# Own buffers for the last three output parts, and a margin before transposes and PV matmuls in the planner's first batch

## Chip, cores and metric

The kernel runs on one core of one Trainium2 chip. The metric is the device time of one execution in microseconds (us), the median of three. A profile of one execution, taken on the same chip, gives a span that is a little shorter than the device time; times inside the trace count from the start of that span.

## What is computed

Block-sparse attention (batch 4, 8 heads, sequence 768, head width 64) and then an MLP-mixer layer on its output. Cut to what matters:

```python
# attention, per batch and head; mask = neighbouring blocks, first and last block, 3 sampled blocks
scores = np.where(mask, q @ k.T / 8, -1e9)
attn = exp(scores - max) / sum
x = attn @ v                          # [4, 768, 512] once the heads stand side by side
# token mixing
u = x + (relu(x.T @ w_tok1) @ w_tok2).T      # 768 -> 256 -> 768, over the sequence
# channel mixing
out = u + relu(u @ w_ch1) @ w_ch2            # 512 -> 1536 -> 512, over the channels
```

Inputs and output are float32; the kernel works in bfloat16 with float32 sums.

## The kernel before

The heads are worked off as 16 pairs (`p` = 0 to 15, four pairs to a batch). For each pair:

- `k`, `q` and `v` are loaded with conversion to bfloat16 (GpSimd's queue, L230, tiles `kraw`, `qraw`, `vraw`), and VectorE rearranges them (L524 `klay`, `qlay`; L521 `vaug`).
- TensorE transposes `klay` and `qlay` (`tk`, `tq`, L575, six matmuls each, for pairs 1 to 9; later pairs use the DMA's transposing path), and VectorE or ScalarE copies the result to `ktb` and `qtb` (L604, or L589 from pair 6 on).
- Nine score steps `(t, jj)` follow. Each has matmuls of keys by queries into the PSUM tile `ps` (L633), one exponential by ScalarE over 128x1024 elements into `et` (L643), and eight PV matmuls of `et` by `vaug` into `po` (L719). After three steps VectorE normalizes (L733 `recip`, L734 into `x`).
- In pairs 0 to 5 the mask rides inside the score matmul as 24 additional rows of `ktb` and `qtb`. From pair 6 on VectorE multiplies `et` by a 0/1 tile `mask` (L651). That tile is built in between by twelve matmuls `pm_mask` (L484) and twelve comparisons (L492).

When two pairs of a batch are complete, token mixing of half the channels runs (`pm_tok`, L797 and L822; VectorE adds into `x`, L830). The result is transposed (`pm_ut`, L851, in the first batch). When a batch is complete, channel mixing runs: 96 matmuls L889 per batch, ReLU into `rc` (L761 ScalarE or L763 VectorE), and the second product L915, which VectorE adds to `u` and stores in `o` (L924, or L931 for partial widths). SyncE's queue writes `o` to memory (L935).

The order on every engine is fixed when the kernel is built. A `Planner` runs a clock of its own (`now`, in ns) over estimated costs. It has streams for TensorE, in order of priority: scores 0, PV 1, mask 1.8, transposes 2, token mixing 3, channel mixing 4. At each moment the first stream whose next item is ready, by the planned times of its inputs and by free PSUM buffers, is put next on TensorE. VectorE, ScalarE and SyncE take from a list of operations in the same way. The planned times only choose an order: on the chip each engine works through its list in that order and waits, by semaphores, for what an instruction really needs. If an instruction's input comes later than planned, everything behind it on its engine waits too.

Buffers that matter here: `ps` 2, `po` 1, `pm` 3 (PSUM, shared by transposes, mask, token and channel mixing), `et` 7, and three rotating output tiles `o`. In the last batch the last 128 rows of the output are cut by channels into parts of 256, 128 and 128, so that only a small piece is left after the last matmul. These parts take their tiles from the same three `o` buffers:

```python
parts[-1:] = [(NC - 1, 0, 256), (NC - 1, 256, 128), (NC - 1, 384, 128)]
...
o = sbw.tile([128, DM], FP32, tag="o", bufs=3, name=f"o{b}_{sc}_{lo}")
```

The functions that the diff touches:

Of the kernel before, what the change touches and what calls it, by code (L numbers as in the profile page):

```python
# [8 lines left out]
FP32 = mybir.dt.float32  # L9
# [41 lines left out]
class Planner:  # L51
# [6 lines left out]


    PE_LAT, SEM = 180.0, 50.0  # L60
    trace = None

    def __init__(self, slots):
# [39 lines left out]
    def step(self):  # L103

        nxt = []
        moved = False
        if self.free_at["pe"] <= self.now:
            for s in self.streams:
                while s[3] is None or (callable(s[3]) and s[3]()):
                    s[3] = next(s[2], False)  # L110
                if s[3] is False or callable(s[3]):
                    continue
                cost, deps, tags, emit, done = s[3]
                t = self.when(deps, tags)
                if t is None:
                    continue
                if t <= self.now:
                    s[3] = None
                    emit()
                    if self.trace is not None:  # L120
                        self.trace.append((self.now, "pe", s[0], cost))
                    self.free_at["pe"] = self.now + cost
                    if done is not None:
                        done.t = self.now + cost + self.PE_LAT + self.SEM
                    moved = True
                    break
                nxt.append(t)
            self.streams = [s for s in self.streams if s[3] is not False]
        else:
            nxt.append(self.free_at["pe"])  # L130
        for eng in ("act", "dve", "sp"):
            if self.free_at[eng] > self.now:
                nxt.append(self.free_at[eng])
                continue
            best = None
            for o in self.ops:
                prio, num, engines, cost, deps, emit, done, lat, tags = o
                if eng not in engines:
                    continue
                if eng == "act" and prio > 0 and self.exp_pending:  # L140
                    continue
                t = self.when(deps, tags)
                if t is None:
                    continue
                if t <= self.now:
                    if best is None or (prio, num) < best[:2]:
                        best = o
                else:
                    nxt.append(t)
            if best is not None:  # L150
                prio, num, engines, cost, deps, emit, done, lat, tags = best
                self.ops.remove(best)
                emit(eng)
                c = cost[eng]
                if self.trace is not None:
                    self.trace.append((self.now, eng, prio, c))
                self.free_at[eng] = self.now + c
                done.t = self.now + c + lat + self.SEM
                moved = True
        if moved:  # L160
            return True
        later = [t for t in nxt if t > self.now]
        if not later:
            return False
        self.now = min(later)
        return True
# [3 lines left out]
def kernel(  # L170
# [17 lines left out]
    DM, DT, DC = 512, 256, 1536  # L188
# [9 lines left out]
    sbw = ctx.enter_context(tc.tile_pool(name="sbw", bufs=2))  # L198
# [13 lines left out]
    P = Planner({"ps": 2, "po": 1, "pm": 3, "et": NET, "a_t": 2, "o": 3, "rc": 2,  # L212
                 "uT": 3})
# [158 lines left out]
    def first_turn(nm, hf):  # L372
        t = psM.tile([128, 3, 128], BF16, tag="pm", name=f"t{nm}first{hf}")
        for c in range(3):
            nc.tensor.matmul(
                out=t[:, c, :], lhsT=lay0[nm][:, 3 * hf + c, :, :].rearrange("p h d -> p (h d)"),
                rhs=ident[:, :], start=(c == 0), stop=(c == 2), is_transpose=True,
            )
        return t

    def first_evac(copy, nm, hf, hd, t):
        buf = (ktb if nm == "k" else qtb)[0]
        copy(
            out=buf[0:64, hd, 384 * hf : 384 * hf + 384],
            in_=t[64 * hd : 64 * hd + 64, :, :].rearrange("p c s -> p (c s)"),
        )
# [9 lines left out]
    def e2_copy(copy, hf, hd, t):  # L396
        copy(out=qtb[0][R, hd, 384 * hf : 384 * hf + 384], in_=t[R, 0:384])
# [27 lines left out]
    def first_rest():  # L425

        def band(eng):
            nc.vector.tensor_copy(out=ktb[0][R, 1, 384:S], in_=indf[:, 384:S])

        P.op(("dve",), {"dve": 250.0}, [], band, prio=0)  # L430
        for nm in ("k", "q"):
            box, last, rel = {}, Ev(), Ev()

            def emit(nm=nm, box=box, rel=rel):
                P.take("pm", rel)
                box["t"] = first_turn(nm, 1)

            yield 330.0, [Ev(START + (200.0 if nm == "k" else 600.0))], [("pm", 1)], emit, last
            for hd in range(2):
                def evac(eng, nm=nm, hd=hd, box=box):  # L440
                    first_evac(vcopy, nm, 1, hd, box["t"])

                ev = P.op(("dve",), {"dve": 350.0}, [last], evac, prio=0)
                f_there[nm, 1].same_as = ev
                rel.same_as = ev
        box, last, rel = {}, Ev(), Ev()

        def emit():
            P.take("pm", rel)
            box["t"] = e2_mm(1, psM, "pm")  # L450

        yield 330.0, [], [("pm", 1)], emit, last
        for hd in range(2):
            def copy(eng, hd=hd, box=box):
                e2_copy(vcopy, 1, hd, box["t"])

            e2_there = P.op(("dve",), {"dve": 420.0}, [last], copy, prio=0)
            rel.same_as = e2_there
        rows_there[0] = e2_there
        for n in range(1, NV):  # L460
            def spread(eng, n=n):
                if eng == "dve":
                    nc.vector.tensor_copy(out=qtb[n][R, :, :], in_=qtb[0][R, :, :])
                else:
                    nc.sync.dma_start(out=qtb[n][R, :, :], in_=qtb[0][R, :, :])

            rows_there[n] = P.op(
                ("dve",) if n == 1 else ("sp",), {"dve": 560.0, "sp": 800.0}, [e2_there], spread,
                prio=1, lat=60.0 if n == 1 else 5000.0,
            )  # L470
# [401 lines left out]
    def ch(b, pool, tag):  # L872
# [4 lines left out]
        for cc in range(12):  # L877
            for sh in range(2):
                last, rel, pbox = Ev(), Ev(), {}
# [28 lines left out]
        for sc, lo, n in parts:  # L908
            last, rel, pbox = Ev(), Ev(), {}
            for cc in range(12):  # L910
                def emit(sc=sc, cc=cc, lo=lo, n=n, rel=rel, pbox=pbox):
                    if cc == 0:
                        P.take("pm", rel)
                        pbox["pm"] = psM.tile([128, DM], FP32, tag="pm", name=f"pm_ch2_{b}_{sc}_{lo}")
                    nc.tensor.matmul(  # L915
                        out=pbox["pm"][:, 0:n], lhsT=box["rc"][:, cc, 128 * sc : 128 * sc + 128],
                        rhs=w_ch2[:, cc, lo : lo + n], start=(cc == 0), stop=(cc == 11),
                    )
                yield n / 2.4 + 2.5, [rc_there[cc, sc // 3], ch2_there[cc // 3]], [("pm", 1)] if cc == 0 else [], emit, last if cc == 11 else None

            def fin(eng, sc=sc, lo=lo, n=n, pbox=pbox):
                o = sbw.tile([128, DM], FP32, tag="o", bufs=3, name=f"o{b}_{sc}_{lo}")
                if n == DM:
                    nc.vector.tensor_tensor(  # L924
                        out=o[:, :].rearrange("p (g e) -> p g e", g=2),
                        in0=pbox["pm"][:, :].rearrange("p (g e) -> p g e", g=2),
                        in1=st[b]["u"][:, :, sc, :], op=ALU.add,
                    )
                else:
                    g, e = lo // 256, lo % 256  # L930
                    nc.vector.tensor_tensor(  # L931
                        out=o[:, 0:n], in0=pbox["pm"][:, 0:n],
                        in1=st[b]["u"][:, g, sc, e : e + n], op=ALU.add,
                    )
                nc.sync.dma_start(  # L935
                    out=APx(out, b * S * DM + sc * DM + lo, [[NC * DM, 128], [1, n]]),
                    in_=o[:, 0:n],
                )

            alias(rel, P.op(("dve",), {"dve": dve_psum(n)}, [last], fin, prio=3))  # L940
        alias(rc_rel, last)

# [81 lines left out]
```

## Time and profile before

| what | value |
|---|---|
| device time, median of 3 | 265.2 us (265.01 to 265.48) |
| span of the profiled execution | 263.8 us |
| TensorE busy | 254.3 us (96%) |
| ScalarE busy | 178.4 us (68%) |
| VectorE busy | 173.1 us (66%) |
| mean granted TensorE clock | 0.993 of full speed |

Two stages with different limits can be told apart. Up to some 195 us attention runs, with token and channel mixing between the scores where they are ready. In the first batch nothing of channel mixing can be ready yet, and ScalarE, with its exponentials, is the busiest engine (10.00 us busy in the stretch from 20 to 30 us). From some 196 us on only channel mixing is left: long runs of L889 and L915 on TensorE. After the last matmul come one VectorE addition and one write to memory.

### The profile page before, as it was taken

How to read it: one execution, taken by the hardware profiler on the slowest of the kernel's cores; microseconds unless marked ns; L12 is line 12 of the kernel's file. 1: busy time of each engine (PE TensorE's matmuls, PEld its weight loads, DVE VectorE, ACT ScalarE, POOL GpSimd, SP SyncE). 2: the span in 40 equal slices, each digit the busy share in tenths (PEclk: the TensorE clock that was granted, in tenths of full speed). 3: DMA queues.
4: the chain of work that ended last, by engine and by line, in shares of the span. 5: the costliest groups of instructions: out<-in, count | busy, mean ns of one | idle time of the engine just before them, and what ended most of it. 6: DMA issues, size and time to landing. Idle time of an engine off the chain costs nothing.

```text
span 263.8 us, 6585 instructions
## 1 busy us (share of the span) xinstructions
PE 254.3 (96%) x2769; PEld 167.2 (63%) x2787; DVE 173.1 (66%) x387; ACT 178.4 (68%) x226; POOL 42.1 (16%) x66
## 2 busy tenths in 40 slices
PE   7899999999999999999999999999999999999993
PEld 3588886898765676567555765666565644565452
DVE  7978968697989789788879798888850013200221
ACT  5789999998887887677777887777317720277000
POOL 8845555462303010000000000000000000000000
PEclk9899999999999999999999999999999999999999
DMA  6999999999665826141734030016214012300122
GB/s 149 183 217 201 213 202 207 204 199 180 90 93 77 105 32 119 43 102 40 176 94 34 2 60 2 2 40 102 81 42 99 0 42 80 121 2 0 48 111 82
DMA packets 39262, 25.58 MB, mean 97 GB/s; under 512 B 20480, under 2 KB 35600, under 8 KB 39232
## 3 DMA queue, kind: packets, MB, share of 16 engines
q0 software_dynamic: 15104, 12.98, 31.6%
q1 hardware_dynamic: 23856, 11.97, 19.4%
q8 instruction: 22, 0.36, 0.6%
q10 hardware_dynamic: 272, 0.20, 0.3%
q14 instruction: 8, 0.07, 0.1%
HBM read 26.74 MB, written 6.29 MB: 125 GB/s over the span
## 4 chain that ended last, share of the span: by engine, by line
PE 87%; DVE 4%; ACT 3%; DMA 2%; issue 1%; SPq 0%; DVEq 0%; ACTq 0%
PE pm_ch L889 24%; PE pm_ch L915 22%; PE ps L633 17%; PE po L719 13%; PE pm_tok L797 4%; PE pm_tok L822 4%; ACT et L643 3%; DMA out_dram<-o 1%; PE tk L575 1%; DMA kf<-in_k_dram 1%; PE pm_mask L484 1%; DVE x L830 1%; DVE et L651 1%; PE tq L575 1%; DVE o L924 0%
## 5 line engine op out<-in xcount | busy, mean ns | idle before, releaser
L643 ACT ACTIVATE et<-ps 128x1024 bf16<-128x1024 f32 x144 | 138.9, 1023 | 29.9 <-PE ps L633 28.9
L889 PE MATMUL pm_ch<-uT,w_ch 128*128 128x384 bf16 x384 | 70.1, 326 | 0.0
L915 PE MATMUL pm_ch<-w_ch,rc 128*128 128x512 bf16 (+2 forms) x294 | 67.0, 362 | 1.1 <-issue 0.3
L633 PE MATMUL ps<-qtb,ktb 64*128 64x256 bf16 (+1 forms) x576 | 61.2, 274 | 1.4 <-ACT et L643 1.2
L719 PEld LDWEIGHTS <-et 128*128 128x128 bf16 x1152 | 49.9, 98 | 16.3 <-issue 3.0
L651 DVE TENSOR_TENSOR et<-et,mask 128x1024 bf16<-128x1024 bf16 x90 | 57.8, 682 | 0.0
L719 PE MATMUL po<-vaug,et 128*128 128x65 bf16 x1152 | 56.3, 194 | 0.6 <-DVE et L651 0.2
L761 ACT ACTIVATE rc<-pm_ch 128x384 bf16<-128x384 f32 x69 | 33.8, 492 | 26.9 <-PE pm_ch L889 26.7
L924 DVE TENSOR_TENSOR o<-pm_ch,x 128x512 f32<-128x512 f32 x23 | 15.8, 687 | 52.6 <-PE pm_ch L915 52.6
L889 PEld LDWEIGHTS <-w_ch 128*128 128x128 bf16 x384 | 35.4, 98 | 22.0 <-issue 2.2
L633 PEld LDWEIGHTS <-ktb 64*128 64x128 bf16 (+1 forms) x576 | 33.0, 96 | 19.4 <-issue 13.9
L915 PEld LDWEIGHTS <-rc 128*128 128x128 bf16 x312 | 27.5, 97 | 24.8 <-issue 1.3
L733 DVE RECIPROCAL recip<-po 128x4 f32<-128x4 f32 x48 | 8.7, 181 | 20.4 <-PE po L719 20.1
L734 DVE TENSOR_TENSOR x<-po,recip 128x256 bf16<-128x256 f32 x48 | 20.4, 424 | 1.7
L830 DVE TENSOR_TENSOR x<-pm_tok,x 128x512 bf16<-128x512 f32 x24 | 15.6, 682 | 4.1 <-PE pm_tok L822 4.1
L230 POOL DMA_DIRECT2D vraw<-in_v_dram x16 | 11.7, 730 | 34.1 <-DVE vaug L521 29.0
L763 DVE TENSOR_SCALAR rc<-pm_ch 128x384 bf16<-128x384 f32 x27 | 14.8, 552 | 2.2 <-PE pm_ch L889 1.8
L822 PE MATMUL pm_tok<-a_t,w_tok 128*128 128x256 bf16 x96 | 14.6, 276 | 0.2
L797 PE MATMUL pm_tok<-x,w_tok 128*128 128x256 bf16 x96 | 13.4, 273 | 0.0
L230 POOL DMA_DIRECT2D kraw<-in_k_dram x15 | 10.8, 718 | 7.8 <-DMA w_tok<-in_moe_w_tok_dram 2.7
L230 POOL DMA_DIRECT2D qraw<-in_q_dram x15 | 10.8, 723 | 6.6 <-DVE klay L524 1.2
L822 PEld LDWEIGHTS <-w_tok 128*128 128x128 bf16 x96 | 9.8, 128 | 1.6 <-issue 1.2
(70 smaller groups left out, 114.4 us busy)
## 6 DMA issues: line engine op xcount, KB each, us to landing
out_dram<-o SPq DMA_DIRECT2D x23, 256.0 KB, 2.1
vraw<-in_v_dram POOLq DMA_DIRECT2D x16, 192.0 KB, 7.3
w_ch<-in_moe_w_ch_dram POOLq DMA_DIRECT2D x8, 384.0 KB, 9.8
kraw<-in_k_dram POOLq DMA_DIRECT2D x15, 192.0 KB, 7.8
qraw<-in_q_dram POOLq DMA_DIRECT2D x15, 192.0 KB, 7.3
w_tok<-in_moe_w_tok_dram POOLq DMA_DIRECT2D x2, 384.0 KB, 10.9
kf<-in_k_dram SPq DMA_DIRECT2D x2, 192.0 KB, 3.2
ktb<-ktb SPq DMA_DIRECT2D x3, 72.0 KB
```

What stands on the lines that cost most here:

```text
L230: nc.gpsimd.dma_start(out=raw[:, :, :, :], in_=APx(src, 2 * p * S * D, [[NC * D, 128], [S * D, 2], [1, NC * D]]),)
L633: nc.tensor.matmul(out=ps[:, hd, 256 * i : 256 * i + 256], lhsT=ktb[n][rows, h, 256 * jj + 128 * i : 256 * jj + 128 * i + 128], rhs=qtb[n] ...
L643: nc.scalar.activation(out=et[:, :, :], in_=ps[:, :, :], func=AF.Exp, scale=0.125)
L651: nc.vector.tensor_tensor(out=ets[s][:, :, :].rearrange("k h (i q) -> k h i q", i=2), in0=ets[s][:, :, :].rearrange("k h (i q) -> k h i q" ...
L719: nc.tensor.matmul(out=po[:, hd, c, :], lhsT=et[:, hd, 256 * i + 128 * c : 256 * i + 128 * c + 128], rhs=va[:, hd, 2 * jj + i, 0:65], star ...
L734: nc.vector.tensor_tensor(out=free(xs[b][:, pb // 2, 2 * t, 128 * (pb % 2) : 128 * (pb % 2) + 128], 0, [[64, 2], [256, 2], [1, 64]],), in0 ...
L761: nc.scalar.activation(out=o(), in_=i, func=AF.Relu)
L797: nc.tensor.matmul(out=box["pm"][:, t, :], lhsT=w_tok1[:, sc, 128 * t : 128 * t + 128], rhs=xs[b][:, g, sc, :], start=(t == 0 and sc == 0) ...
L822: nc.tensor.matmul(out=ubox["pm"][:, i, :], lhsT=w_tok2[:, t, :, 2 * s2 + i], rhs=a_t[:, t, :], start=(i == 0 and t == 0), stop=(i == 1 an ...
L830: nc.vector.tensor_tensor(out=st[b]["u"][:, g, 2 * s2 : 2 * s2 + 2, :], in0=ubox["pm"][:, :, :], in1=xs[b][:, g, 2 * s2 : 2 * s2 + 2, :], ...
L889: nc.tensor.matmul(out=pbox["pm"][:, 0:384], lhsT=w_ch1[:, dmc, 128 * cc : 128 * cc + 128], rhs=st[b]["uT"][:, dmc // 2, 3 * sh : 3 * sh + ...
L915: nc.tensor.matmul(out=pbox["pm"][:, 0:n], lhsT=box["rc"][:, cc, 128 * sc : 128 * sc + 128], rhs=w_ch2[:, cc, lo : lo + n], start=(cc == 0 ...
```

## The change

There are three edits. The first lets the planner, while its clock is below 40 us, treat items of the streams with priority 1.8 and 2 (mask, transposes) as ready only 300 ns after the planned time of their inputs, and PV items (priority 1) 100 ns after. What is put next in such a moment is whatever else is ready. The second raises the planned VectorE cost of one small copy in the start-up from 420 to 555 ns. The third gives the three partial output tiles a tag of their own with three buffers of 256 columns. The purpose of the first two is an order in which TensorE is held up less by inputs that come late; that of the third is that the last tiles need not wait for earlier ones to be written.

```diff
     PE_LAT, SEM = 180.0, 50.0
+    tight = 40e3
...
                 t = self.when(deps, tags)
                 if t is None:
                     continue
+                if self.now < self.tight:
+
+                    t += 300.0 if 1.5 < s[0] < 2.5 else 100.0 if s[0] == 1 else 0.0
                 if t <= self.now:
...
-            e2_there = P.op(("dve",), {"dve": 420.0}, [last], copy, prio=0)
+            e2_there = P.op(("dve",), {"dve": 555.0}, [last], copy, prio=0)
...
-                o = sbw.tile([128, DM], FP32, tag="o", bufs=3, name=f"o{b}_{sc}_{lo}")
+                if n == DM:
+                    o = sbw.tile([128, DM], FP32, tag="o", bufs=3, name=f"o{b}_{sc}_{lo}")
+                else:
+                    o = sbw.tile([128, 256], FP32, tag="olast", bufs=3, name=f"o{b}_{sc}_{lo}")
```

In the built programs the order changes on TensorE and VectorE from the first transposes of pair 1 up to the transposes `pm_ut` and the token mixing of the first batch (some 70 us in the trace of before). From there on both programs have the same order, except for the output buffers. One copy, `ktb` from the transposes of pair 9, moves from VectorE to ScalarE. The queues of SyncE and GpSimd keep their order. No instruction is added or removed.

## Prediction

> **What bounds the kernel now.** I read four views in this order: the page (engine sums and slices), the chain of waits that ended last, the timelines of the two ends of the kernel, and the waits by engine.
>
> ```profile
> PE 254.3 (96%) x2769; PEld 167.2 (63%) x2787; DVE 173.1 (66%) x387; ACT 178.4 (68%) x226; POOL 42.1 (16%) x66
> PEclk9899999999999999999999999999999999999999
> PE 87%; DVE 4%; ACT 3%; DMA 2%; issue 1%; SPq 0%; DVEq 0%; ACTq 0%
> ```
>
> TensorE is the bound as a whole (87% of the chain). But it is not loaded alike everywhere, and both edits sit at ends where something else decides. First the tail: the timeline from 255 us (start, length, engine, line; in brackets the idle time before and what ended it) and the end of the chain.
>
> ```profile
> 254.78 4.54 PE L915 MATMUL pm_ch<-w_ch,rc 128*128 128x512 bf16 x44
> 256.71 0.69 DVE L924 TENSOR_TENSOR o<-pm_ch,x 128x512 f32<-128x512 f32 x1 [1.90 <-PE pm_ch L915]
> 258.02 0.42 DVE L931 TENSOR_TENSOR o<-pm_ch,x 128x256 f32<-128x256 f32 x1 [0.62 <-PE pm_ch L915]
> 258.69 0.29 DVE L931 TENSOR_TENSOR o<-pm_ch,x 128x128 f32<-128x128 f32 x1 [0.25 <-PE pm_ch L915]
> 260.94 0.29 DVE L931 TENSOR_TENSOR o<-pm_ch,x 128x128 f32<-128x128 f32 x1 [1.96 <-DMA out_dram<-o]
> ```
> ```profile
> 256.71 0.70 DVE o L924
> 257.43 3.39 DMA out_dram<-o
> 260.82 0.03 issue
> 260.85 0.05 DVEq L931
> 260.89 0.04 issue
> 260.94 0.29 DVE o L931
> ```
>
> The last matmul ends at 254.78+4.54 = 259.32, yet the last addition starts at 260.94: it waits for the write of the tile three before it, the 256 KB tile filled at 256.71, which lands at 260.82. The chain goes through that write, not through TensorE. Now the head.
>
> ```profile
> 9.00:10.00 1.00, 0.33 (x2) 0.16 (x2) 0.97 (x3) 1.00 (x2) 0.96 (x3) 1.00 1.24 185
> 11.00:12.00 1.00, 1.00 (x10) 0.82 (x8) 0.94 (x4) 0.71 (x1) 0.66 (x1) 0.50 1.35 201
> 12.00:13.00 1.00, 1.00 (x17) 0.94 (x16) 0.99 (x2) 0.56 (x1) 0.68 (x2) 0.50 1.22 179
> 13.00:14.00 1.00, 1.00 (x17) 0.88 (x15) 0.58 (x4) 0.46 (x1) 0.73 (x2) 0.50 1.34 207
> ```
> ```profile
> 12.44 1.02 ACT L643 ACTIVATE et<-ps 128x1024 bf16<-128x1024 f32 x1 [0.73 <-PE ps L633]
> 14.52 22.45 ACT L643 ACTIVATE et<-ps 128x1024 bf16<-128x1024 f32 x24 [1.06 <-PE ps L633]
> ```
>
> The columns of the first view are the stretch, its length, busy time of PE, PEld, DVE, ACT and POOL, granted clock, DMA share and GB/s. From 11 to 14 us TensorE runs at half clock and ScalarE starves (0.73 and 1.06 us idle, both waiting for score matmuls). Then 24 exponentials run without a gap, 22.45/24 = 0.935 us each: to 37 us ScalarE sets the pace, and TensorE has time to spare.
>
> **What the Trainium skill says.** "TensorE: Matmul & The Clock Gate", part 1, "What's actually happening": TensorE's clock is halved after a mostly idle window of about 3.4 us and comes back after a busy one; the window runs freely. The trace agrees: 0.33 us busy in the slice at 9 us, then 0.50 for some 3.2 us. Same page, part 2, "Step-by-step: what each phase is for": matmuls stay in program order, only weight loads are pulled ahead. So a PV group whose `vaug` is late holds up the scores behind it; 24 PV matmuls take 1.32 us in the chain between 12.40 and 13.72 here. "DMA: Bandwidth & Descriptors", "Anatomy of one DMA": a fixed part of about 2 us per transfer, mostly the receipt of the last write. The trace has 2.3 us for the 64 KB writes at the end, 2.6 for 128 KB and 3.4 for 256 KB: a reused tile is blocked for that long.
>
> **Part by part.**
>
> *Own tiles for the last parts.* The 1.96 us wait goes. The second partial addition started at 258.69, 0.02 to 0.03 us after its product; the last part is 12 matmuls of 128 columns, at a quarter of the 0.219 us that 512 columns take in the chain (10.74 us for 49), so 12 x 0.055 = 0.66. Its product is there at 259.33, which agrees with the end of TensorE. The addition then starts at 259.36 instead of 260.94: 1.58 us earlier. From its end to the end of the span before: 263.8 - 261.23 = 2.57 us. This write now overlaps three others in flight. If it is as quick as before, the gain is 1.58; if it takes the 3.4 us of the slowest row, the gain is 1.58 - 0.83 = 0.75. All four writes are 512 KB, and the densest 0.2 us slices of the tail move 350 to 390 GB/s, about 1.5 us of data from 258.15 on, when the engines start on the first; so the last 64 KB is hardly queued. I take 1.5. The bigger reservation in SBUF costs no time.
>
> *Margin and 555 ns, start-up.* These move work, they add none. The first difference in the built order is around the second score step. Before: 6 `tk`, scores (0,1,1), 24 PV, scores (0,1,2), with `vaug` of pair 0 ahead of `qlay` on VectorE. After: 5 `tk`, scores (0,1,1), 1 `tk`, 3 `tq`, 8 PV, scores (0,1,2), 16 PV. VectorE takes `qlay` first, then `vaug` of pairs 0 and 1, then `ktb`. TensorE is idle before this in both, so I take the half clock as unchanged, with four scores at 0.85 us and a transposition at 0.11. One transposition less ahead of (0,1,1): its end moves from 12.40 to about 12.3. Then 4 transposes 0.43, 8 PV (a third of 1.32) 0.44, four scores 0.85: 14.0 instead of 14.50. The exponential that started at 14.52 starts at about 14.05. The next needs its scores behind 16 PV, about 0.5, and four scores, 0.5: 15.1, where it started at 14.52+0.94 = 15.46. ScalarE is thus 0.4 us ahead, and since it runs without gaps to 37 us the lead stays. Of the other waits that the reordering brings: `ktb` of pair 1 is copied behind `vaug` of pair 1 (about 12.8 instead of 12.0), which nobody needs before the scores of pair 1 at some 17 us; `vaug` of pair 3 stands ahead of `ktb` and `recip` of pair 1, and its load can hold VectorE. GpSimd's queue went on at 23.53 after a wait for a `vraw` load, by its place the one of pair 3, so up to 0.6 us is lost on VectorE; the exponentials have one step in hand there.
>
> *36 to 64 us.* ScalarE has five gaps, 1.7 us in all: four of about 0.2 while the mask is built, and one of 0.84 at 62.3. After, two `pm_tok` groups move between the mask matmuls and the masks are spread further; the copy of `ktb` for pair 9 goes to ScalarE (0.74 us planned) and falls into the 0.84 gap. Against it, `klay` and `qlay` of pair 6 come ahead of a mask comparison, and their loads landed shortly before 37.6 and 38.5. I take this stage at zero, with 0.5 us either way.
>
> *From 70 us on.* Order equal, chain almost all TensorE, so a lead of 0.4 us passes through to the end.
>
> Sum: 265.2 - 1.5 - 0.4 = 263.3 us.
>
> **Rivals.**
>
> 1. The tail gains, the head gives nothing: the lead is eaten by loads, whose rate is near 200 GB/s from 10 to 62 us and which do not come sooner. For it: one VectorE wait on `kraw` at 21.27 exists. Against: it is 0.29 us. 265.2 - 1.5 = 263.7.
> 2. The head gains more: of the four small mask gaps (0.84 us) and the start, 1.2 in all. 265.2 - 1.5 - 1.2 = 262.5. Against: nothing in the trace says the gaps come from mask matmuls alone.
> 3. The new order stalls: `vaug` of pair 3 and `klay`, `qlay` of pair 6 hold VectorE, `po` (one buffer) comes late and ScalarE starves for 1 to 1.5 us. With the tail's gain: about 265.0, no difference.
> 4. Slower: those stalls at their full size (0.6 at 23 us, 0.8 and 0.7 at 37 us) and a second half-clock stretch of 3.2 us, which costs up to 1.6: 3.7 us lost in part, say 2.3. 265.2 - 1.5 + 2.3 = 266.0. Against: VectorE shows one wait on a load in the whole head, and no TensorE gap of a microsecond after 11 us.
>
> **How the numbers follow.** Forecast 0.50, rival 1 0.22, rival 2 0.13, rival 3 0.08, rival 4 0.07. The bound for no change is 0.5 us (0.2%). Faster: the first three, 0.85. Same: 0.08. Slower: 0.07. The range holds forecast and rival 1, the pessimistic write at the end (0.75 less gain gives 264.1 to 264.4), and rival 2: 262.3 to 264.6. Rivals 3 and 4 are left out.
>
> **What would show it.** Right: the last L931 starts within 0.1 us of the last matmul with no wait on a write; the long run of exponentials starts near 14.1. The copy of `ktb` for pair 9 lies in ScalarE's gap, and the first run of 96 L889 starts about 0.4 us before 196.73. Wrong: VectorE waits on `vraw` or `kraw` near 23 or 37 us, ScalarE gaps above 0.5 us between 15 and 37 us, a second stretch at clock 0.50, or more than 3 us from the last addition to the end.

## Result, and the profile after

The changed kernel takes 263.5 us (263.41 to 263.62, 4 executions) against 265.1 us before: ratio 0.9941, 95% interval 0.9923 to 0.9958. A second set of ten executions gave 263.27 us against 264.82 us: 0.9945 (0.9926 to 0.9964). The forecast was 263.3 us. Three executions of the kernels below are left out of all medians, ratios and counts, one of no_margin (268.46 us), one of pv_only (268.63 us) and one of v3_fill (365.72 us, its clock at 0.65 in every stretch from 5 us on).

Inserted lines shift the source: L924 and L931 became L931 and L938, L643 became L647, L719 L723, L734 L738, L521 L525, L524 L528, L889 and L915 L893 and L919.

The page of the changed kernel, engine sums, clock and chain:

```profile
PE 253.7 (97%) x2769; PEld 166.3 (63%) x2787; DVE 172.2 (66%) x386; ACT 179.4 (69%) x227; POOL 42.0 (16%) x66
...
PEclk9999999999999999999999999999999999999999
...
PE 85%; DMA 6%; DVE 4%; POOL 2%; issue 1%; POOLq 0%
```

TensorE is still the bound. ScalarE has one instruction more, the copy for pair 9. The 6% of DMA in the chain are new; they are explained below. The tail, first the timeline, then the end of the chain:

```profile
255.93 0.69 DVE L931 TENSOR_TENSOR o<-pm_ch,x 128x512 f32<-128x512 f32 x1 [1.90 <-PE pm_ch L919]
257.24 0.42 DVE L938 TENSOR_TENSOR o<-pm_ch,x 128x256 f32<-128x256 f32 x1 [0.62 <-PE pm_ch L919]
257.91 0.29 DVE L938 TENSOR_TENSOR o<-pm_ch,x 128x128 f32<-128x128 f32 x1 [0.25 <-PE pm_ch L919]
258.58 0.29 DVE L938 TENSOR_TENSOR o<-pm_ch,x 128x128 f32<-128x128 f32 x1 [0.38 <-PE pm_ch L919]
```
```profile
254.00 4.55 PE pm_ch L919 x44
258.56 0.02 issue
258.58 0.29 DVE o L938
```

The last addition now waits for the matmuls alone (0.38 us) and starts 0.03 us after the last one. The head, clock and busy time by microsecond (columns as in the prediction: PE, PEld, DVE, ACT, POOL, clock), then ScalarE's exponentials:

```profile
11.00:12.00 1.00, 0.97 (x12) 0.71 (x12) 0.97 (x3) 0.93 (x2) 0.67 (x1) 1.00 1.30 197
12.00:13.00 1.00, 1.00 (x19) 0.91 (x20) 0.97 (x3) 1.00 (x2) 0.72 (x1) 1.00 1.28 187
```
```profile
7.81 1.02 ACT L647 ACTIVATE et<-ps 128x1024 bf16<-128x1024 f32 x1 [0.88 <-PE ps L637]
9.10 16.25 ACT L647 ACTIVATE et<-ps 128x1024 bf16<-128x1024 f32 x17 [0.27 <-PE ps L637]
25.96 16.70 ACT L647 ACTIVATE et<-ps 128x1024 bf16<-128x1024 f32 x17 [0.62 <-PE ps L637]
```

The half clock of 11 to 14 us is absent in this execution, and ScalarE's two gaps there with it. In their place there is a gap of 0.62 us at 25.96.

The difference of the spans, 263.8 - 261.9 = 1.9 us, splits at the first run of 96 matmuls of channel mixing: it starts at 195.95 instead of 196.73, so 0.78 us come from the head and 1.12 from the tail. The two executions differ in their clock too: before had a mean of 0.993, the changed kernel 1.00. What this does to the 0.78 is taken up below.

### The profile page after: what moved, and what is told of

It is laid out like the page before. It is cut to its first block, busy times and chain, and to the rows that moved or that the text cites. A ratio compares the mean times of both kernels' runs of the same rounds, so it can differ in the third digit from the quotient of the medians.

```text
span 261.9 us, 6584 instructions
## 1 busy us (share of the span) xinstructions
PE 253.7 (97%) x2769; PEld 166.3 (63%) x2787; DVE 172.2 (66%) x386; ACT 179.4 (69%) x227; POOL 42.0 (16%) x66
## 4 chain that ended last, share of the span: by engine, by line
PE 85%; DMA 6%; DVE 4%; POOL 2%; issue 1%; POOLq 0%
PE pm_ch L893 24%; PE pm_ch L919 23%; PE ps L637 15%; PE po L723 13%; DMA vraw<-in_v_dram 6%; PE pm_tok L801 4%; PE pm_tok L826 4%; PE pm_mask L488 1%; DVE x L834 1%; DVE et L655 1%; PE tk L579 1%; PE tq L579 1%; PE pm_ut L855 0%; DVE x L738 0%; DVE ktb L608 0%
## 5 line engine op out<-in xcount | busy, mean ns | idle before, releaser
L647 ACT ACTIVATE et<-ps 128x1024 bf16<-128x1024 f32 x144 | 139.1, 1024 | 28.0 <-PE ps L637 26.7
L893 PE MATMUL pm_ch<-uT,w_ch 128*128 128x384 bf16 x384 | 70.1, 326 | 0.0
L919 PE MATMUL pm_ch<-w_ch,rc 128*128 128x512 bf16 (+2 forms) x294 | 67.0, 362 | 1.1 <-issue 0.3
L637 PE MATMUL ps<-qtb,ktb 64*128 64x256 bf16 (+1 forms) x576 | 60.4, 272 | 1.1 <-ACT et L647 0.7
L723 PEld LDWEIGHTS <-et 128*128 128x128 bf16 x1152 | 49.3, 97 | 17.0 <-issue 3.1
L723 PE MATMUL po<-vaug,et 128*128 128x65 bf16 x1152 | 56.1, 193 | 1.2 <-DVE x L738 0.8
L931 DVE TENSOR_TENSOR o<-pm_ch,x 128x512 f32<-128x512 f32 x23 | 15.8, 687 | 52.6 <-PE pm_ch L919 52.6
L893 PEld LDWEIGHTS <-w_ch 128*128 128x128 bf16 x384 | 35.4, 98 | 22.0 <-issue 2.2
L919 PEld LDWEIGHTS <-rc 128*128 128x128 bf16 x312 | 27.5, 98 | 24.8 <-issue 1.3
L738 DVE TENSOR_TENSOR x<-po,recip 128x256 bf16<-128x256 f32 x48 | 20.4, 424 | 1.7
```

What stands on the lines that cost most here:

```text
L637: nc.tensor.matmul(out=ps[:, hd, 256 * i : 256 * i + 256], lhsT=ktb[n][rows, h, 256 * jj + 128 * i : 256 * jj + 128 * i + 128], rhs=qtb[n] ...
L647: nc.scalar.activation(out=et[:, :, :], in_=ps[:, :, :], func=AF.Exp, scale=0.125)
L723: nc.tensor.matmul(out=po[:, hd, c, :], lhsT=et[:, hd, 256 * i + 128 * c : 256 * i + 128 * c + 128], rhs=va[:, hd, 2 * jj + i, 0:65], star ...
L738: nc.vector.tensor_tensor(out=free(xs[b][:, pb // 2, 2 * t, 128 * (pb % 2) : 128 * (pb % 2) + 128], 0, [[64, 2], [256, 2], [1, 64]],), in0 ...
L893: nc.tensor.matmul(out=pbox["pm"][:, 0:384], lhsT=w_ch1[:, dmc, 128 * cc : 128 * cc + 128], rhs=st[b]["uT"][:, dmc // 2, 3 * sh : 3 * sh + ...
L919: nc.tensor.matmul(out=pbox["pm"][:, 0:n], lhsT=box["rc"][:, cc, 128 * sc : 128 * sc + 128], rhs=w_ch2[:, cc, lo : lo + n], start=(cc == 0 ...
```

## The experiments

Each kernel ran in up to five rounds beside the kernel before, four kernels to a set; each set had its own chip. "Before" is the median of the same set. The last column counts executions with a low clock: a granted TensorE clock, as a mean over the execution, below 0.9965. The others are called executions at full clock. One stretch at half clock like that of 11 to 14 us (3.4 us) takes 0.0065 from the mean of 264 us, which gives 0.993 or 0.994. Only the mean is known of an execution without a trace; 8 of the 55 of the kernel before stand at 0.996.

| kernel | median us | before | ratio (95% interval) | low clock |
|---|---|---|---|---|
| before, three sets | | 265.09, 264.82, 265.10 | | 55 of 151 |
| changed, again | 263.27 | 264.82 | 0.9945 (0.9926 to 0.9964) | 1 of 10 |
| tail_only | 263.93 | 265.09 | 0.9954 (0.9938 to 0.9969) | 6 of 20 |
| head_only | 264.39 | 265.09 | 0.9991 (0.9974 to 1.0008) | 10 of 22 |
| v3_later | 263.25 | 265.09 | 0.9951 (0.9928 to 0.9975) | 5 of 11 |
| landings | 264.59 | 265.09 | 0.9985 (0.9970 to 1.0000) | 2 of 22 |
| fill | 263.39 | 264.82 | 0.9934 (0.9907 to 0.9961) | 0 of 7 |
| v3_fill | 262.96 | 264.82 | 0.9922 (0.9894 to 0.9949) | 0 of 5 |
| v3_fill_again | 263.11 | 265.10 | 0.9924 (0.9904 to 0.9944) | 0 of 6 |
| no_margin | 265.22 | 264.82 | 1.0018 (1.0002 to 1.0035) | 7 of 21 |
| no_555 | 264.15 | 265.10 | 0.9972 (0.9958 to 0.9986) | 12 of 20 |
| tr_only | 263.84 | 265.10 | 0.9954 (0.9939 to 0.9970) | 13 of 22 |
| pv_only | 265.82 | 265.10 | 1.0032 (1.0020 to 1.0044) | 12 of 21 |

### The tail alone

```diff
 (kernel before)
-                o = sbw.tile([128, DM], FP32, tag="o", bufs=3, name=f"o{b}_{sc}_{lo}")
+                if n == DM:
+                    o = sbw.tile([128, DM], FP32, tag="o", bufs=3, name=f"o{b}_{sc}_{lo}")
+                else:
+                    o = sbw.tile([128, 256], FP32, tag="olast", bufs=3, name=f"o{b}_{sc}_{lo}")
```

> Only the own output tiles, head as before. Theory (the tail wait was 1.58 us, and the last write then takes about 0.46 us longer because it follows closer on three others): 1.0 to 1.5 us faster than before, 263.6 to 264.1 us, granted clock as low as before (0.993), last addition within 0.1 us of the last matmul. Rival (the gain of the whole change comes from the head, the writes end when they end): 265.0 to 265.2 us.

Measured: 263.93 us, 1.16 us faster than before. The theory holds, the rival falls: the larger part of the gain is the tail. In its trace the last addition starts at 259.25, 0.03 us after the last matmul. One part of the expectation failed: only 6 of 20 executions have a low clock. At full clock the medians are 263.70 and 264.78, a gain of 1.08 us.

The expectation put the missing part of the 1.58 us on a last write that takes longer. From the start of its issue to the end of the span, however, it takes about 2.6 us in both kernels. The queue of SyncE shows where the time went. First before, then the changed kernel; start and length of the instructions that issue the writes:

```profile
258.47 0.33 SPq L935 DMA_DIRECT2D out_dram<-o  x1
```
```profile
257.69 1.00 SPq L942 DMA_DIRECT2D out_dram<-o  x1
...
259.26 0.40 SPq L942 DMA_DIRECT2D out_dram<-o  x1
```

In the changed kernel SyncE took 1.00 us to issue the 128 KB write, where before it took 0.33. The two issues behind it slid, and the last write was issued at 259.26 although its addition ended at 258.58 + 0.29 = 258.87. From that end to the end of the span are 3.03 us here, 2.57 before. In v3_fill_again (the last of the kernels below that beat the changed one) the last issue follows its addition at once, in 0.33 us, and the rest is 260.7 - 258.13 = 2.57 us again. Its last addition, and its last issue:

```profile
257.84 0.29 DVE L947 TENSOR_TENSOR o<-pm_ch,x 128x128 f32<-128x128 f32 x1 [0.38 <-PE pm_ch L928]
```
```profile
258.16 0.33 SPq L951 DMA_DIRECT2D out_dram<-o  x1
```

So the wait on the buffer had partly turned into a wait in the issuing queue. The length of the long issue follows the 256 KB write ahead of it. That write lands 3.2 us after its issue began in the changed kernel, 2.6 in fill and 3.4 in v3_later; the issue behind it takes 1.00, 0.35 and 1.16 us, and ends 1.2 us before that landing in all three. In the kernel before, where it was the third issue that took longer (0.68 us), it ends 1.1 us before. What holds the issue, and why that write is slower in some executions, stays open. Issuing the parts from two queues was not tried.

### The head alone

```diff
 (changed kernel)
-                if n == DM:
-                    o = sbw.tile([128, DM], FP32, tag="o", bufs=3, name=f"o{b}_{sc}_{lo}")
-                else:
-                    o = sbw.tile([128, 256], FP32, tag="olast", bufs=3, name=f"o{b}_{sc}_{lo}")
+                o = sbw.tile([128, DM], FP32, tag="o", bufs=3, name=f"o{b}_{sc}_{lo}")
```

> Only the planner's margin and the 555 ns, the last parts share the three output tiles as before. Theory (the head gives 0.77 us at 196 us, and the half-clock stretch at 11 us goes because TensorE is held up less): 264.2 to 264.5 us, granted clock 0.999 or above in every run. Rival (the missing half-clock stretch was chance of that execution): the clock is 0.993 in some runs and 1.00 in others, and times spread by more than 0.5 us. Rival (head worth nothing): 265.0 to 265.2 us.

Measured: 264.39 us, median 0.7 us lower, but the ratio's interval (0.9974 to 1.0008) includes no change. The median lies in the theory's range, but the theory on the clock falls and its rival holds: 10 of 22 executions have a low clock, as 55 of 151 have in the kernel before. The changed order does not keep the half clock away. At full clock the medians are 264.22 and 264.78: the head gives 0.56 us. In the low-clock executions it is 265.17 against 265.41.

### The load that took the lead away

The changed kernel at 15 us was well ahead of the old one, but not at 36. VectorE between 21 and 25 us, and TensorE behind it:

```profile
20.89 0.36 DVE L528 COPY klay<-kraw 128x768 bf16<-128x768 bf16 x1 [0.54 <-DMA kraw<-in_k_dram]
...
22.89 0.36 DVE L525 COPY vaug<-vraw 128x768 bf16<-128x768 bf16 x1 [0.60 <-DMA vraw<-in_v_dram]
23.16 1.11 DVE L608 COPY ktb<-tk 64x768 bf16<-64x768 bf16 x2
24.31 0.18 DVE L737 RECIPROCAL recip<-po 128x4 f32<-128x4 f32 x1
24.53 0.42 DVE L738 TENSOR_TENSOR x<-po,recip 128x256 bf16<-128x256 f32 x1
```
```profile
25.01 0.42 PE L723 MATMUL po<-vaug,et 128*128 128x65 bf16 x8 [0.79 <-DVE x L738]
```

`vaug` of pair 3, which nobody needs for another ten microseconds, waits 0.60 us for its load. Behind it stand `ktb` and the normalization of pair 1. `po` has one buffer, so PV and all scores behind it wait 0.79 us, and ScalarE runs dry for 0.62 us. The chain that ended last goes through this load, which makes the 6% of DMA. The planner believed in an earlier landing. The load of `kraw` shown in the first line was late too, and that matters: in the trace of head_only, which has the same order here, `vaug` also waits (0.62 us), but `kraw` was there in time. PV then waits only 0.22 us and ScalarE has no gap. One line plans this load 1.5 us later:

```diff
 (changed kernel)
+            if (nm, p) == ("v", 3):
+                arr = Ev(arr.t + 1.5 * US)
             deps = [arr]
```

> The changed kernel, with the load of vraw for pair 3 planned 1.5 us later: on VectorE that one copy moves behind the two ktb copies of pair 3, nothing else moves. Theory (the copy waited 0.60 us for its load and held up the normalization, PV and so ScalarE, which then had a gap of 0.62 us at 25.96): the gap goes, ScalarE is 0.4 to 0.6 us ahead, 262.9 to 263.1 us. Rival (the stage up to 40 us is bound by the rate of loads, and the next late load takes the lead away): 263.4 to 263.6 us, with the wait back at kraw of pair 6 near 37 us.

Measured: 263.25 us in all. Five of its eleven executions have a low clock; the six others have a median of 263.04, 1.74 us below the kernel before at full clock (264.78), where the changed kernel is 1.39 below (263.22 against 264.61). This fits the theory, with 0.35 us instead of 0.4 to 0.6, but the two differences come from two sets. Two kernels of one set that differ in this copy alone point the same way: fill and v3_fill, described below, have 263.39 and 262.96 us. Neither difference is clear of the spread (the seven executions of fill lie between 262.56 and 263.84), so the theory is supported, not shown. The timeline of ScalarE in v3_later has no gap from 15.05 to 40 us. It can't settle the point, because it is from an execution at low clock, in which ScalarE comes 1 us later to this place:

```profile
15.05 24.98 ACT L649 ACTIVATE et<-ps 128x1024 bf16<-128x1024 f32 x26 [0.68 <-PE ps L639]
```

Then the same for all loads:

```diff
 (changed kernel)
-    dma = {"free": 7.6 * US}
+    dma = {"free": 9.0 * US}
```

> The changed kernel, with all loads planned 1.4 us later (first free time of the loads 9.0 instead of 7.6 us), which is how late the loads of pair 3 landed in the trace. Theory (late loads hold up VectorE in three places, 0.54, 0.60 and 0.35 us): no wait of VectorE on a load above 0.3 us, 262.6 to 263.2 us. Rival (another order brings other waits of the same size, since the plan is wrong in more than the loads): 263.3 to 264.5 us.

Measured: 264.59 us, a little beyond the rival's range; the rival holds. ScalarE's start is as hoped (31 exponentials without a gap from 8.49 to 38 us), but the planner then wrote another order for the whole kernel, and between 65 and 70 us TensorE is busy only 4.00 of 5 us, against 4.66 in the changed kernel. A correct model of one cost does not give a better order everywhere.

### The half clock

```diff
 (changed kernel, in scores(), after the matmuls)
+        if s == (0, 0, 2):
+            fill = psO.tile([128, 512], FP32, tag="po", name="fill")
+            for _ in range(4):
+                nc.tensor.matmul(
+                    out=fill[:, :], lhsT=free(one[:, 0:1], 0, [[0, 128]]),
+                    rhs=free(one[:, 0:1], 0, [[0, 512]]), start=True, stop=True,
+                )
```

> The changed kernel once more, for more executions. If the half-clock stretch near 11 us comes and goes by execution, as in the runs with only one part: some executions with a granted clock below 0.996, near 264.5 us, the rest near 263.5. If the changed order avoids it: all at 0.998 or above, 263.4 to 263.7 us.

> The changed kernel with four dummy matmuls of 512 columns after the scores (0,0,2), in the stretch where TensorE is idle near 9.5 us; their product is never read. If the half-clock stretch comes from that idle time: no execution below 0.998, and the median equals that of the undisturbed executions, 263.4 to 263.6 us. If it has another cause: the same share of executions at low clock as the changed kernel. If the dummies delay the scores behind them: 0.1 to 0.3 us slower.

> The dummy matmuls and the later copy of vraw for pair 3 together. If both act and add up: clock 0.998 or above in every execution, 262.9 to 263.1 us, faster than either kernel. If the dummies do nothing: two groups of executions, near 263.0 and 264.1 us.

> Dummy matmuls and the later copy of vraw for pair 3 once more, for more executions and an undisturbed trace. If it beats the changed kernel: 262.8 to 263.0 us, ratio to before near 0.993, no execution with clock below 0.998, and no gap of ScalarE above 0.4 us between 15 and 37 us. If the first set was chance: 263.2 to 263.5 us.

Measured: with the dummies none of 18 executions in the three sets had a low clock, where at the rate of the kernel before some six would. Without them, the kernels with the same order on TensorE had it in 16 of 47 (changed 1 of 14, head_only 10 of 22, v3_later 5 of 11), and the kernel before in 55 of 151. So matmuls in the idle time near 9.5 us remove the low clock. The idle time alone does not decide, though: in its trace landings is as idle there (TensorE busy 0.30 us in the slice from 9 to 10 us), but it had a low clock in 2 of 22, where the three other changed kernels of its set had it in 21 of 53. In the next slice its TensorE is busy 1.00 us, against 0.74 in the kernel before; whether this is the reason was not tested.

At full clock fill has 263.39 us and the changed kernel 263.22 in the same set; this 0.17 us is within the spread, so a cost of the dummies is neither shown nor excluded. Together with the later `vaug` they give 262.96 and 263.11 us, the lowest medians of the table; the second missed its expected 262.8 to 263.0 by 0.1. v3_later at full clock, without dummies, is as fast (263.04). The slice at 9 us of v3_fill_again:

```profile
9.00:10.00 1.00, 0.98 (x6) 0.39 (x4) 0.99 (x2) 1.00 (x2) 1.00 (x3) 1.00 1.22 187
```

TensorE is busy 0.98 us there instead of 0.33. In the kernel before, the full-clock and low-clock executions of the first set differ by 265.41 - 264.78 = 0.63 us.

### Margin and planned cost taken apart

```diff
 (changed kernel; each line alone; the names behind # are added here)
+    tight = 0.0                                             # no_margin
+    e2_there = P.op(("dve",), {"dve": 420.0}, ...)          # no_555
+    t += 300.0 if 1.5 < s[0] < 2.5 else 0.0                 # tr_only
+    t += 100.0 if s[0] == 1 else 0.0                        # pv_only
```

> The changed kernel without the margin: the 555 ns and the own output tiles stay. If the margin carries the gain of the head: at equal clock as slow as the own tiles alone, 263.6 to 263.8 us undisturbed. If the 555 ns carry it: 263.4 to 263.5 us undisturbed. If the order from the 555 ns alone is worse than that of before: above 263.9 us.

> The changed kernel with the old 420 ns: margin and own output tiles alone. If the margin is what helps the head, with or without the 555 ns: 263.0 to 263.5 us at full clock, like the changed kernel. If margin and 555 ns only work together: near the own tiles alone, 263.5 to 264.0 us. If the gain is the luck of one order among many: anything from 263 to 265 us.

> The changed kernel with the margin for mask and transposes alone, none for PV. Without the margin TensorE stood 1.11 us at 14 us before transposes of pair 2 whose klay was late; if that is the wait that matters, this keeps the gain: 263.0 to 263.6 us, no wait of TensorE on klay above 0.3 us. If PV's margin matters as much: 263.8 to 264.5 us.

> The changed kernel with the margin for PV alone. The built order has the transposes of pairs 1 and 2 ahead of the first PV, as without any margin, so TensorE should stand before klay of pair 2 again: 264.5 to 265.3 us. If PV's margin is what matters: 263.0 to 263.6 us.

Medians at full clock, of 8 to 14 executions, each less that of the kernel before in the same set: tail_only -1.08, no_555 263.79 - 264.86 = -1.07, tr_only 263.67 - 264.86 = -1.19, changed -1.39, no_margin 264.95 - 264.61 = +0.34, pv_only 265.46 - 264.86 = +0.60. Less the tail, then: the margin with the old 420 ns gives the head nothing. With 555 ns and no margin for transposes the head loses 1.4 to 1.7 us. With both, and PV's margin, it gains some 0.3. The losses are clear of the spread; differences of 0.3 us or less, among them what PV's margin is worth (0.2), are not. By the expectations, then, the order from the 555 ns alone is worse than that of before, and no_555 fits the reading that margin and 555 ns only work together; tr_only lies between its two forecasts, pv_only above both. The timeline of TensorE in no_margin shows what the margin is for:

```profile
11.91 1.30 PE L637 MATMUL ps<-qtb,ktb 88*128 88x256 bf16 x8
14.32 0.51 PE L579 MATMUL tk<-ident,klay 128*128 128x128 bf16 x6 [1.11 <-DVE klay L528]
...
15.05 0.65 PE L723 MATMUL po<-vaug,et 128*128 128x65 bf16 x16
```

The transposes of pair 2 are put on TensorE at the moment for which `klay` is planned; it comes 1.11 us late, and the scores stand behind them, so that ScalarE is without an exponential from 14.49 to 16.24. PV could not have gone ahead: VectorE copies its `vaug` only from 14.56 on. Why pv_only is slower than forecast stays open. Its order has the same early transposes, but its only trace is of the execution that took 268.63 us, and there the longest wait of TensorE is 1.0 us for `x`, not for `klay`.

## Why the prediction was right, point by point

ScalarE's waits from 36 to 64 us, which the fourth point needs, before and after: total, number of waits and the longest of them.

```profile
ACT et L643 <- PE ps L633: 1.7, 5, 0.8
```
```profile
ACT et L647 <- PE ps L637: 0.4, 2, 0.2
```

- *Own tiles.* The step was right in its mechanism and its first term: the addition starts 0.03 us after the last matmul (forecast 259.36 against 259.33). The mis-sized term is the write after it: 3.03 us to the end instead of the 2.65 that go with a gain of 1.5, so the tail gave 1.12 us in the profiled pair, and 1.08 in tail_only at full clock. It was counted as contention of transfers; what the trace shows is SyncE's issue at 0.39 us after the addition's end.
- *Start-up.* The forecast assumed the half clock unchanged. That assumption was wrong for the profiled execution of the changed kernel, where it is absent; it comes and goes in both kernels. The sixth exponential starts at 13.10 instead of 14.52, a lead of 1.4 us rather than 0.4, but much of it is the clock's and not the order's. In v3_later, which has the changed order here and a half clock of the same length that began 0.6 us later, the sixth exponential starts at 13.36, but the seventh at 15.05 (forecast 15.1) against 15.44 before, and of these 0.39 us 0.24 stand at the first exponential already. The forecast also read the slice at 9 us as agreeing with a mostly idle window of about 3.4 us. The trace of before shows no such window: from 7 to 11 us TensorE is idle 0.95 us of 4.
- *The lead stays.* Wrong. In the profiled pair the 29th exponential starts at 35.58 against 35.95: of 1.4 us 0.4 are left. The gap at 25.96 took 0.7 of the lead. The rest went in stretches without a gap, where ScalarE took 0.96 and 0.98 us for an exponential instead of 0.935. At equal low clock nothing is left: v3_later starts its 29th at 35.87, before at 35.95 and tail_only at 35.84. The step had named `vaug` of pair 3, with up to 0.6 us on VectorE (measured 0.60), and dismissed it because ScalarE has a step in hand. With that wait alone (head_only) this is about right; with `kraw` late as well it is not, and the single `po` passes the wait on. This is what rival 3 described, at a smaller size.
- *36 to 64 us at zero.* At equal clock this is where the lead arose. ScalarE waits 1.7 us in five gaps there before, and 0.4 in two after (the lines above). The copy of pair 9 fell into the gap at 62 us as forecast, and of the four small gaps of the mask stage two are left. The 54th exponential starts 0.7 us earlier in the profiled pair (60.57 against 61.27), so this stage gave 0.3 us. In the single traces at equal low clock it gave as much: v3_later, which differs from the changed kernel in one copy on VectorE, is at 60.87, against 61.27 before and 61.16 in tail_only. That is within the 0.5 that were allowed, but it is what rival 2 saw in the mask gaps, at about half its size, and not the forecast's step.
- *From 70 us on.* Right: 0.69 us at 62 us, 0.78 at 196.

That the sum of the forecast, 1.9 us, equals that of the profiled pair is luck. The parts, 0.4 of head and 1.5 of tail, were 0.78 and 1.12, and the pair sets an execution at low clock against one at full clock, which alone is worth 0.63 us in the kernel before. At full clock on both sides the whole change gives 1.39 us, the tail 1.08, and the head 0.3 (changed less tail_only) to 0.56 us (head_only). This fits the forecast's 0.4 in size, near the limit of what these runs can tell, but the traces at equal clock put it into the mask stage rather than the start-up. Three signs that the forecast had named for being wrong came true: a wait on `vraw` near 23 us, a gap of ScalarE above 0.5 us before 37 us, and just over 3 us from the last addition to the end.

## What to carry to other kernels

Look at the last buffer rotation of a kernel: a tile that is reused behind a store of 2 to 3 us can put that store on the chain, even when TensorE is busy to the end; small tiles of their own gave 1.1 us here. In an order written by a planner, an operation whose input is a load is best planned after the operations that others wait for: here a copy of data that were needed much later waited 0.60 us, behind another load that was 0.54 us late, and VectorE, TensorE and ScalarE stopped in turn. Planning all loads later made another order for the whole kernel, which lost more than it gained. And take several executions before reading a start-up, and compare them at equal clock: here one execution in three had a low clock, with the old order and with the new one, and the first pair of traces gave the order a lead that was in large part the clock's.

## What the runs showed of the hardware that was not expected

- A mean TensorE clock below 0.9965 came in 55 of 151 executions of one and the same program. In the traces of before, tail_only and v3_later it is one stretch of 3.4 us at half clock, after a slice in which TensorE was busy 0.3 to 0.4 us of one and, before that slice, 0.8 us or more. Four dummy matmuls of 512 columns in that place went with none in 18. An equally idle slice with denser work behind it (landings) went with 2 in 22.
- The issue of a write on SyncE's queue took 0.33 or 0.34 us for 22 of the 26 writes of the kernel before. The issue behind the last 256 KB write took 0.33 to 1.16 us in the traces that are compared here. Where it was long it ended 1.2 us before that write landed, and the issues behind it slid.
